# Query sketches of batch 0 on 32x64 tiles, with the heads of a pair swapped by half groups, and a new order

## The chip, the cores and the metric

The kernel runs on one core of a Trainium2 chip. The metric is device time in microseconds, as the median of three runs. The profile is of one further execution of the same program.

## What is computed

Polynomial-sketch attention without softmax, followed by a feed-forward stage (FFN). Batch is 4, heads 4, sequence 1088, head dimension 32, sketch size r = 8; the FFN has 4352 tokens, width 128 and inner width 2048.

```python
def phi(x):                                   # 8 x 8 = 64 features per token and head
    a = np.einsum('rd,bhsd->bhsr', S1, x)
    b = np.einsum('rd,bhsd->bhsr', S2, x)
    return np.einsum('bhsi,bhsj->bhsij', a, b).reshape(*x.shape[:-1], r * r)
q_p, k_p = (phi(q), phi(k))
kv = np.einsum('bhsf,bhsd->bhfd', k_p, v)
z = np.sum(k_p, axis=2)
num = np.einsum('bhsf,bhfd->bhsd', q_p, kv)
den = np.einsum('bhsf,bhf->bhs', q_p, z)[..., None] + 1e-06
# x = (num / den), heads side by side, as 4352 tokens of 128
r = np.maximum(x @ w_in, 0.0)
out = (r * r) @ w_out
```

## The kernel before

The kernel builds a graph of named operations and then emits them in the order of a list, `PLAN`. Each word of the list is `name:engine` and, where it allocates, `:slot`. Every engine works through its own operations in the order in which they stand in the list; an operation at the head of an engine's queue that waits for another engine holds all that stand behind it there. DMA issues take their place in the queue of SP, ACT (ScalarE) or POOL (GpSimd). A word `+12` puts twelve filler matmuls (L328) into TensorE's queue. The list was written out by a planner, which also picks engines where an operation has several (`r`, `g`, `kve`, `ab`, `xe`, `vp`, some `qp`) and the slots of PSUM and SBUF.

The names, for batch b:

- `ldk`, `ldq`, `ldv`: loads of k, q and v (L366 to L392). `vin` has two buffers, so that v of batch 2 goes where v of batch 0 was.
- `tk`, `tq`: 32x32 block transposes of k and q on VectorE (L417, L419, L541). Batch 0 has q in two parts, `tq0.0` and `tq0.1`.
- `ksk`, `ka`, `kp`: sketches of k on TensorE (L458), a copy of the first factor to SBUF on ScalarE (L467), the product of the two on VectorE, for the last piece of batch 0 on GpSimd (L477).
- `vp`: v copied beside a column of ones (L430, L433). `kv`: key features times v, summed over tokens on TensorE (L497). `kve`: its copies from PSUM to SBUF, by pairs of heads; `kvz` holds the two heads of a pair in their places, `kvs` holds them swapped (L515, L517).
- `qr`, `qa`, `qp`: sketches of q repeated to 64 features per head, copy of one factor (`qa`, L567), product (`qp`, L571).
- `num`, `mx`, `tx`, `xe`: query features times state (L793), division by the denominator on VectorE (L806 to L816), transposes on TensorE (L827), copy to `xT` (L831).
- `m1.n.m`, `r`, `g`, `m2`, `oe`, `st`: FFN block n: first product (L858), ReLU (L870 on ScalarE, L872 on VectorE), square (L883, L885), second product (L900), transpose of the result (L910), store (L929). Blocks have 256, 7 times 512, 256 and 256 tokens; block 0 needs only the first group of batch 0.
- `gate`, `win`, `wout`: three loads each of the FFN weights on the GpSimd queue, converted to bf16 on the way; all wait for the gate, a copy that waits for k of batch 0 (L397 to L404). The first two are half as large as the third.

`MODE` gives each batch its way to make the query features: batch 0 "full", batch 1 "half", batches 2 and 3 "rep".

In mode "full" the groups of batch 0 have 320, 384 and 384 columns (`QGROUPS`). Per group and pair of heads there are two matmuls, one for each factor, on a tile of 64 rows and 128 columns. Their weights `SF` are the repeated sketch matrix under a block mask of the two heads, made on GpSimd (L283, L287). In mode "half" of batch 1 one factor is repeated by DMA (`qr1`, `ab1`, `rd1`), the other by matmuls `qb1` on tiles of 32 rows and 64 columns with the weights `SR` (L693). There the heads of a pair are swapped in every second piece of columns, and `num` takes `kvs` in place of `kvz` for these.

The order around the change, in the list before, by engine from the start to the first FFN evacuation on VectorE:

```
PE  ksk0.0-2 qr0.0 ksk1.1 +3 kv0.0-2 qr0.1 num0.0 ksk1.0 qr1 qr0.2 tx0.0 num0.1 m1.0.1 num0.2 tx0.1 m1.0.3 m1.0.0 kv1.0 tx0.2 m1.0.2 qr2 ...
DVE ST tk0.0 mkz mk ident SK tk0.1 SKs tq0.0 tk1.0 kp0.0 kp0.1 qp0.0.0 qp0.0.1 tq0.1 kp1.1 tq1.0 qp0.1.0-1 mx0.0 kp1.0 xe0.0 qp0.2.0-1 mx0.1 mx0.2 tq2.0 xe0.1 xe0.2 r.0.2
```

Of the kernel before, what the change touches and what calls it, by code (L numbers as in the profile page):

```python
# [43 lines left out]
ldk0.0:SP S0:ACT iota:POOL heat0:PE ldk0.1:SP S1:ACT heat4:PE ldk0.2:SP heat2:PE ldq0.0:ACT ldk1.1:SP heat1:PE warm:ACT ldk1.0:SP heat6:PE heat5:PE  # L44
heat7:PE heat3:PE ldv0.0:SP ST:DVE tk0.0:DVE ldv0.1:SP ldv0.2:SP mkz:DVE mk:DVE gate:POOL win0:POOL ldv0.3:SP ident:DVE SK:DVE ldv0.4:SP tk0.1:DVE
SF:POOL +12 ksk0.0:PE:b0 ldq0.1:SP SKs:DVE ksk0.1:PE:b1 ldq1.1:SP tq0.0:DVE SR:POOL ksk0.2:PE:b2 qr0.0:PE:p3,p5 z0:POOL ka0.2:ACT ka0.1:ACT ka0.0:ACT
ldq1.0:SP tk1.0:DVE ldv1.4:SP kp0.2:POOL ldv1.0:SP qa0.0.1:ACT:A0 qa0.0.0:ACT:A1 kp0.0:DVE ldv1.2:SP ksk1.1:PE:b2 ldv1.3:SP vp0.0:POOL ldv1.1:SP
ka1.1:ACT kp0.1:DVE win1:POOL vp0.1:ACT +3 kv0.0:PE:b0 win2:POOL qp0.0.0:DVE wout0:POOL qp0.0.1:DVE kv0.1:PE tq0.1:DVE z1:POOL kv0.2:PE kp1.1:DVE
wout1:POOL ldq2.0:SP qr0.1:PE:p3,p5 kve0.0:ACT kve0.1:ACT ldq2.1:SP tq1.0:DVE num0.0:PE:b1 qa0.1.0:ACT:A2 qa0.1.1:ACT:A1 qp0.1.0:DVE ksk1.0:PE:b0
ldq3.1:SP qp0.1.1:DVE ldk2.0:SP qr1:PE:b2 ka1.0:ACT mx0.0:DVE:den0 ldv2.2:SP qr0.2:PE:p3,p5 ab1.0:ACT ab1.1:ACT rd1.0.1:SP kp1.0:DVE vp1.0:POOL  # L50
rd1.0.0:SP vp1.1:POOL tx0.0:PE qa0.2.0:ACT:A0 rd1.1.0:SP num0.1:PE:b2 xe0.0:DVE qa0.2.1:ACT:A2 qp0.2.0:DVE ldk2.1:SP wout2:POOL qp0.2.1:DVE
m1.0.1:PE:p0 mx0.1:DVE:den1 rd1.1.1:SP num0.2:PE:b3 r.0.1:ACT:r0 ldk3.1:SP tx0.1:PE mx0.2:DVE:den2 m1.0.3:PE:p4 m1.0.0:PE:p0 r.0.3:ACT:r1 ldk3.0:SP
tq2.0:DVE kv1.0:PE:b6 rd1.3.1:SP r.0.0:ACT:r2 rd1.3.0:SP xe0.1:DVE tx0.2:PE m1.0.2:PE:p4 xe0.2:DVE rd1.2.0:SP g.0.0:ACT:g0 qr2:PE:p0 r.0.2:DVE:r3
rd1.2.1:SP m1.1.2:PE:p2 ab2:ACT ldq3.0:SP g.0.2:DVE:g1 m1.1.3:PE:p4 g.0.1:ACT:g2 wr2.3:SP r.1.2:DVE:R4 m1.1.6:PE:p0 kv1.1:PE r.1.3:ACT tk2.0:DVE
r.1.6:ACT:R6 qb1.0:PE:p2,p4 wr2.2:SP g.0.3:ACT:g3 m2.0.0:PE:b7 qp1.0.0:DVE m1.1.0:PE:p0 ldv2.1:SP kve1.1:DVE kve1.0:ACT m2.0.1:PE kve1.3:DVE ldv2.0:SP
kve1.2:DVE r.1.0:ACT:R2 qp1.0.1:DVE m1.1.4:PE:p2 wr2.1:SP tk3.0:DVE ksk2.0:PE:b6 r.1.4:ACT:R0 wr2.0:SP qb1.1:PE:p4,p0 ldv2.3:SP g.1.3:ACT:G4 m2.0.2:PE
qp1.1.0:DVE m1.1.1:PE:p2 ldv2.4:SP qp1.1.1:DVE m2.0.3:PE m1.1.5:PE:p4 oe0:DVE:osb0 ka2.0:ACT r.1.1:ACT num1.0:PE:p0 kp2.0:DVE rdA2.0:SP r.1.5:ACT
tq3.0:DVE rdB2.0:SP ksk2.1:PE:b2 g.1.1:ACT:G6 num1.1:PE:b3 vp2.1:POOL mx1.0:DVE:den0 ksk3.1:PE:b6 g.1.5:ACT:G0 mx1.1:DVE:den1 qr3:PE:p4 st0.0.1:SP
tx1.0:PE ab3:DVE tx1.1:PE ka2.1:ACT m2.1.0:PE:b7 xe1.0:ACT xe1.1:DVE wr3.1:SP m1.1.7:PE:p4 kp2.1:DVE vp2.0:ACT ldv3.3:SP m2.1.1:PE wr3.2:SP r.1.7:ACT
# [916 lines left out]
```

## Time and profile before

| | |
|---|---|
| median of the runs | 111.94 us (111.84 to 114.46) |
| profiled execution | 111.21 us, of it span 109.4 us |
| granted TensorE clock | 1.0 |
| TensorE busy | 102.8 us (94%) |
| VectorE busy | 92.3 us (84%) |
| ScalarE busy | 85.2 us (78%) |
| GpSimd busy | 23.5 us (21%) |
| moved by DMA | 16.33 MB |

The span runs from the first to the last instruction. Busy time of TensorE counts pipelined matmuls to their modelled end. In the views by time a row gives the start, the length, the engine, the line, the operation, the operands and the count; a note in brackets at its end is the idle time just before it, with what ended it. Neighbouring rows of one engine may overlap a little, so the distance of two starts is the better price of an instruction that follows another without a gap.

### The profile page before, as it was taken

What the parts mean: (1) busy time and instruction counts of PE and PEld (TensorE: products, weight loads), DVE (VectorE), ACT (ScalarE), POOL (GpSimd) and SP (SyncE); (2) the same over time, 40 slices, a digit from 0 to 9 for tenths busy, and PEclk for the clock granted to TensorE, in tenths of its full rate; (3) what the DMA queues carried; (4) which work ended last, traced back from release to release, by engine and by line L of the source; (5) the groups of instructions that cost most, each with busy time, mean ns of one, the idle gap of its engine ahead of it and who ended that gap; (6) DMA issues with size and microseconds to landing.
All of it is one profiled execution on the core that took longest, in us unless ns stands there. A gap on an engine that the chain in (4) does not pass through costs nothing.

```text
span 109.4 us, 3331 instructions
## 1 busy us (share of the span) xinstructions
PE 102.8 (94%) x1343; PEld 61.8 (57%) x1343; DVE 92.3 (84%) x141; ACT 85.2 (78%) x105; POOL 23.5 (21%) x45
## 2 busy tenths in 40 slices
PE   7999999999989999999999989999999999999940
PEld 2365864875646955555854435558544544657620
DVE  0199999999899989987998999987999999888540
ACT  0507246399999989998999999991789999999900
POOL 1257918000002103394320505500000000000000
PEclk9999999999999999999999999999999999999999
DMA  1999999999973777546596554450022033143252
GB/s 31 274 327 303 300 208 311 311 267 297 205 247 91 210 210 210 168 116 193 160 235 181 175 151 78 68 96 6 0 46 41 6 57 51 21 75 68 39 88 48
DMA packets 29727, 16.33 MB, mean 149 GB/s; under 512 B 20368, under 2 KB 26896, under 8 KB 29712
## 3 DMA queue, kind: packets, MB, share of 16 engines
q1 hardware_dynamic: 27744, 14.82, 51.7%
q0 software_dynamic: 992, 1.05, 5.8%
q10 hardware_dynamic: 976, 0.26, 1.2%
q8 instruction: 10, 0.16, 0.6%
q14 instruction: 5, 0.04, 0.1%
HBM read 13.27 MB, written 2.79 MB: 147 GB/s over the span
## 4 chain that ended last, share of the span: by engine, by line
PE 62%; DMA 14%; ACT 8%; SPq 6%; DVE 4%; issue 2%; ACTq 1%; POOL 1%; DVEq 0%; POOLq 0%
PE psum L858 20%; PE psum L900 18%; PE psum L793 8%; ACT rraw L870 6%; PE psum L497 6%; DMA vin<-in_v_dram 5%; DMA out_dram<-osb 5%; DMA S_sb<-in_S_dram 3%; PE psum L557 3%; SPq L929 2%; PE psum L827 2%; SPq L741 2%; PE psum L711 2%; DMA scr<-ab 2%; ACT graw L883 2%
## 5 line engine op out<-in xcount | busy, mean ns | idle before, releaser
L870 ACT ACTIVATE rraw<-psum 128x1024 bf16<-128x1024 f32 x51 | 49.4, 1030 | 3.0 <-PE psum L858 2.8
L900 PE MATMUL psum<-graw,w_out 128*128 128x512 bf16 (+1 forms) x160 | 39.3, 347 | 0.6
L858 PE MATMUL psum<-xT,w_in 128*128 128x512 bf16 (+1 forms) x160 | 38.8, 348 | 0.4 <-DVE rraw L872 0.4
L885 DVE TENSOR_TENSOR graw<-rraw 128x1024 bf16<-128x1024 bf16 (+1 forms) x30 | 26.8, 922 | 1.3 <-ACT rraw L870 1.2
L883 ACT ACTIVATE graw<-rraw 128x1024 bf16<-128x1024 bf16 (+1 forms) x18 | 25.6, 1437 | 0.2
L858 PEld LDWEIGHTS <-w_in 128*128 128x128 bf16 x160 | 17.4, 114 | 13.0 <-issue 1.3
L900 PEld LDWEIGHTS <-w_out 128*128 128x128 bf16 x160 | 15.0, 97 | 14.4 <-issue 3.4
L872 DVE TENSOR_SCALAR rraw<-psum 128x1024 bf16<-128x1024 f32 x17 | 20.6, 1219 | 1.6 <-PE psum L858 0.8
L754 POOL TENSOR_TENSOR qp<-qp,Bq 128x384 f32<-128x384 f32 (+1 forms) x9 | 11.6, 1297 | 19.6 <-PE psum L858 6.8
L477 DVE TENSOR_TENSOR kp<-psum,ka 128x1024 f32<-128x1024 f32 (+2 forms) x8 | 10.1, 1268 | 0.0
L793 PE MATMUL psum<-kvz,qp 128*64 128x66 f32 (+1 forms) x252 | 9.6, 223 | 0.0
L793 PEld LDWEIGHTS psum<-kvz,qp 128*64 128x64 f32 (+1 forms) x252 | 8.4, 136 | 1.8 <-ACT A L567 0.5
L497 PEld LDWEIGHTS psum<-vp,kp 128*32 128x32 f32 (+1 forms) x432 | 7.2, 118 | 2.5 <-issue 1.0
L910 DVE STREAM_TRANSPOSE osb<-psum 128x512 f32<-128x512 f32 (+1 forms) x10 | 6.3, 633 | 2.4 <-PE psum L900 2.2
L497 PE MATMUL psum<-vp,kp 128*32 128x33 f32 (+1 forms) x432 | 7.9, 207 | 0.2 <-POOL vp L430 0.2
L328 PE MATMUL psum<-const-bfloat16-1.0 128*128 128x512 bf16 x23 | 7.0, 466 | 0.8 <-PEq L960 0.8
L430 POOL COPY vp<-vin 128x512 f32<-128x512 f32 x5 | 3.0, 615 | 21.0 <-DMA vin<-in_v_dram 21.0
L467 ACT COPY ka<-psum 128x128 f32<-128x128 f32 (+3 forms) x9 | 2.3, 274 | 5.7 <-PE psum L458 5.7
L458 PEld LDWEIGHTS psum<-SK,kT 128*64 128x64 f32 x144 | 5.0, 137 | 2.2 <-DVE kvs L517 0.9
L458 PE MATMUL psum<-SK,kT 128*64 128x64 f32 x144 | 5.8, 225 | 0.4 <-DVE kvs L517 0.4
L541 DVE STREAM_TRANSPOSE qT<-qin 128x1088 f32<-128x1088 f32 (+2 forms) x5 | 5.4, 1072 | 0.1
L417 DVE STREAM_TRANSPOSE kT<-kin 128x1024 f32<-128x1024 f32 (+1 forms) x5 | 5.1, 1020 | 0.1
(63 smaller groups left out, 70.7 us busy)
## 6 DMA issues: line engine op xcount, KB each, us to landing
...
```

Of the source, the lines that this page charges most:

```text
L328: nc.tensor.matmul(tiles["b7"][:, 0:n], ones(128), ones(n), start=True, stop=True)
L458: nc.tensor.matmul(o[32 * g : 32 * g + 32 * gw, :, j - j0, :], lhsT, SK.rearrange("p x h r -> p x (h r)"), start=True, stop=True)
L477: (nc.gpsimd if ke == "POOL" else nc.vector).tensor_tensor(out=kp[i][:, j0:j1].rearrange("p j h (x y) -> p (j h) x y", y=R), in0=bb[:, :, ...
L497: nc.tensor.matmul(t[p : p + fw, 33 * (h // 2) : 33 * (h // 2) + 33], kp[i][:, j, h, f : f + fw], vp[i][:, h, j, :], start=(j == 0 and h < ...
L754: (nc.gpsimd if e == "POOL" else nc.vector).tensor_tensor(out=qp[i][:, pr, t0 : t0 + n], in0=qp[i][:, pr, t0 : t0 + n], in1=Bq[i][:, pr, t ...
L793: nc.tensor.matmul(t[32 * cc : 32 * cc + 32 * m, lo:hi], lhsT, We[:, hf] if part == 2 else w[:, part].rearrange("p m d -> p (m d)"), start ...
L858: nc.tensor.matmul(at(hb)[:, step * w : step * w + N], w_in[:, 512 * (ct // E) : 512 * (ct // E) + 512].rearrange("p (c e) -> p e c", e=E) ...
L870: nc.scalar.activation(o, h, ACTF.Relu)
L872: nc.vector.tensor_scalar_max(o, h, 0.0)
L883: nc.scalar.activation(at(gb)[:, 0:w2], r, ACTF.Square)
L885: nc.vector.tensor_tensor(out=at(gb)[:, 0:w2], in0=r, in1=r, op=ALU.mult)
L900: nc.tensor.matmul(at(ob)[:, 0:N], w_out[:, ct, :], at(gb)[:, lo + N * w : lo + N * w + N], start=(ct == 0), stop=(ct == CT - 1))
```

## The change

Batch 0 goes from mode "full" to mode "pe" (which the code has; the functions are unchanged). Per group, the columns are cut in two halves. For each factor, half and head there is one matmul on a tile of 32 rows and 64 columns, with the plain repeated matrix `SR` as weights: 16 matmuls of half the columns in place of 4. In the first half a head writes the PSUM partitions of its own place in the pair, in the second half those of the other, so that the eight tiles of one factor are all different. `SF` is not made any more. For the swapped half `num0` takes `kvs`, so `kve0` has four copies in place of two.

```diff
-MODE = ("full", "half", "rep", "rep")
+MODE = ("pe", "half", "rep", "rep")
```

The sketches that this puts in the place of L557, and their copies and products:

```python
for x in range(2):
    for half in range(2):
        for h in range(H):
            lo = 64 * ((h % 2) ^ half)
            nc.tensor.matmul(
                at(hb[h // 2])[lo : lo + 64, 512 * half + 256 * x : 512 * half + 256 * x + n],
                SR[32 * h : 32 * h + 32, x].rearrange("p x y -> p (x y)"),
                qT[i][32 * h : 32 * h + 32, t0 + n * half : t0 + n * half + n], start=True, stop=True)
```

The list `PLAN` is new as a whole. By engine, the part up to the first FFN evacuation on VectorE:

```
PE   ksk0.0-2 qr0.0 qr1 +3 kv0.0-2 qr0.1 num0.0 ksk1.0 +1 num0.1 qr0.2 tx0.0 ksk1.1 tx0.1 m1.0.2 m1.0.1 num0.2 kv1.0 m1.0.0 m1.0.3 tx0.2 kv1.1 ...
DVE  mkz ST mk tk0.0 tk0.1 SK tq0.0 tq1.0 SKs kp0.0 kp0.1 ident qp0.0.0 ab1.1 tq0.1 kve0.3 kve0.0 qp0.0.1 tk1.0 qp0.1.0-1 mx0.0 kp1.0 mx0.1 qp0.2.1-0 xe0.1 kp1.1 mx0.2 tq2.0 r.0.0
ACT  ka0.0-2 qa0.0.0 vp0.1 qa0.0.1 ab1.0 kve0.1 kve0.2 qa0.1.1-0 ka1.0 qa0.2.1 xe0.0 qa0.2.0 vp1.0 ka1.1 r.0.2 ...
POOL gate win1 wout1 z0 iota SR win0 vp0.0 win2 kp0.2 wout0 z1 vp1.1 wout2 ...          (before: iota gate win0 SF SR z0 kp0.2 vp0.0 win1 win2 wout0 z1 wout1 vp1.0 vp1.1 wout2)
SP   ldk0.0-2 ldq1.1 ldq1.0 ldv0.0-4 ldq0.1 ldk1.0 ldk1.1 ldv2.3 ldv1.0 ldv1.1 ldv2.4 rd1.1.0 ldv1.3 ldv1.2 ldv1.4 ldq2.1 ldq2.0 ...
     (before: ldk0.0-2 ldk1.1 ldk1.0 ldv0.0-4 ldq0.1 ldq1.1 ldq1.0 ldv1.4 ldv1.0 ldv1.2 ldv1.3 ldv1.1 ldq2.0 ...)
```

Over the whole list VectorE has 13 of the 68 `r` in place of 17, and 13 of the squares of 2048 columns in place of 12, 19 of those of 1024 in place of 18; ScalarE has the rest. The groups, tile sizes, buffers and the number of fillers at the start (8, then 15 in the list, in another division) are otherwise the same.

More of the change, by code (lines that the diff above doesn't have):

```diff
@@ L43 @@
 PLAN = """
[L44 to L59, printed above, removed]
@@ L84 @@
[L84 to L87 removed]
+mkz:DVE ldk0.0:SP S0:ACT heat0:PE ldk0.1:SP S1:ACT heat5:PE ldk0.2:SP heat3:PE ldq0.0:ACT ldq1.1:SP heat7:PE warm:ACT ldq1.0:SP heat1:PE heat2:PE
@@ new lines @@
+heat4:PE heat6:PE ldv0.0:SP ldv0.1:SP ldv0.2:SP gate:POOL ST:DVE win1:POOL mk:DVE ldv0.3:SP tk0.0:DVE wout1:POOL ldv0.4:SP tk0.1:DVE z0:POOL ldq0.1:SP
+ldk1.0:SP SK:DVE tq0.0:DVE iota:POOL +11 ksk0.0:PE:b0 SR:POOL ldk1.1:SP tq1.0:DVE ksk0.1:PE:b1 ka0.0:ACT win0:POOL ksk0.2:PE:b2 ka0.1:ACT
+qr0.0:PE:p3,p5 ka0.2:ACT SKs:DVE kp0.0:DVE qa0.0.0:ACT:A0 qr1:PE:b2 vp0.0:POOL vp0.1:ACT win2:POOL kp0.1:DVE +3 kv0.0:PE:b0 kp0.2:POOL qa0.0.1:ACT:A1
+ldv2.3:SP ident:DVE ab1.0:ACT qp0.0.0:DVE ldv1.0:SP kv0.1:PE ab1.1:DVE ldv1.1:SP wout0:POOL tq0.1:DVE ldv2.4:SP kv0.2:PE z1:POOL rd1.1.0:SP kve0.3:DVE
```

67 lines of the change are left out of this document (39 added, 28 removed).

## The prediction

> **What bounds the kernel now.** I read the page first (busy shares and slices), then busy time by stretches, then the order of time on each engine through the first 28 us, since every removed or added instruction lies there.
>
> ```profile
> PE 102.8 (94%) x1343; PEld 61.8 (57%) x1343; DVE 92.3 (84%) x141; ACT 85.2 (78%) x105; POOL 23.5 (21%) x45
> ...
> DMA  1999999999973777546596554450022033143252
> ```
> ```profile
> 10.00:15.00 5.00, 4.82 (x95) 3.29 (x93) 4.93 (x7) 2.37 (x8) 3.48 (x10) 1.00 1.09 294
> ...
> 30.00:35.00 5.00, 4.45 (x68) 2.77 (x66) 4.74 (x9) 5.00 (x6) 0.04 (x1) 1.00 0.63 190
> ...
> 60.00:70.00 10.00, 9.63 (x183) 5.12 (x182) 9.96 (x12) 9.85 (x11) 4.74 (x3) 1.00 0.51 130
> ```
>
> TensorE is busy 94% of the span, but that row counts pipelined matmuls from start to modelled end, so it overstates the need for TensorE. VectorE is the telling column at the front (the columns are TensorE, its weight loads, VectorE, ScalarE, GpSimd): 4.93 of 5 us between 10 and 15 us, while ScalarE has 2.37. The DMA slices stand at 9 from 2.7 to 27 us. So the attention of batch 0, which has to end before the feed-forward stage can run, is held by VectorE's queue with DMA behind it; later all three engines are near full. The order of time shows how tight VectorE is:
>
> ```profile
> 5.00 0.24 DVE L251 STREAM_TRANSPOSE ST<-S_sb 128x64 f32<-128x64 f32 x1 [5.00 <-DMA S_sb<-in_S_dram]
> ...
> 8.05 1.25 DVE L417 STREAM_TRANSPOSE kT<-kin 128x1024 f32<-128x1024 f32 x1
> ...
> 9.35 2.05 DVE L477 TENSOR_TENSOR kp<-psum,ka 128x1024 f32<-128x1024 f32 x2
> 11.32 0.87 DVE L571 TENSOR_TENSOR qp<-psum,A 128x320 f32<-128x320 f32 x2
> 12.11 0.96 DVE L541 STREAM_TRANSPOSE qT<-qin 128x768 f32<-128x768 f32 x1
> 13.00 1.45 DVE L477 TENSOR_TENSOR kp<-psum,ka 128x1280 f32<-128x1280 f32 x1
> 14.52 1.31 DVE L541 STREAM_TRANSPOSE qT<-qin 128x1088 f32<-128x1088 f32 x1
> 15.75 0.98 DVE L571 TENSOR_TENSOR qp<-psum,A 128x384 f32<-128x384 f32 x2
> 16.66 0.15 DVE L814 TENSOR_SCALAR den<-psum 128x12 f32<-128x12 f32 x1
> ...
> 17.59 1.22 DVE L477 TENSOR_TENSOR kp<-psum,ka 128x1024 f32<-128x1024 f32 x1
> 18.80 0.32 DVE L831 COPY xT<-psum 128x320 bf16<-128x320 bf16 x1
> 19.04 1.01 DVE L571 TENSOR_TENSOR qp<-psum,A 128x384 f32<-128x384 f32 x2
> 19.97 0.16 DVE L814 TENSOR_SCALAR den<-psum 128x12 f32<-128x12 f32 x1
> ...
> 24.13 1.23 DVE L872 TENSOR_SCALAR rraw<-psum 128x1024 bf16<-128x1024 f32 x1 [0.15 <-PE psum L858]
> ```
>
> From the first transpose at 5.00 (it waits for the sketch matrices, which stay) to the first FFN evacuation at 24.13 no row of this engine but the last has an idle note, nor have those left out here. The differences of starts are the prices used below: k transpose of batch 1 1.30 (8.05 to 9.35), the two key products 1.97, a pair of query products 0.79 (320 columns) or 0.91 to 0.93 (384), q transposes 0.89 (768) and 1.23 (1088), the key product of 1280 1.5, that of 1024 1.2, a normalisation 0.93 (16.66 to 17.59), the copy of a transposed group 0.24 to 0.32.
>
> ```profile
> 8.19 1.35 PE L557 MATMUL psum<-qT,SF 64*128 64x320 f32 x8
> ...
> 11.21 2.29 PE L497 MATMUL psum<-vp,kp 128*64 128x33 f32 x72 [0.18 <-POOL vp L430]
> 13.43 1.56 PE L557 MATMUL psum<-qT,SF 64*128 64x384 f32 x8
> ...
> 20.10 0.92 PE L793 MATMUL psum<-kvz,qp 128*64 128x66 f32 x24
> 21.04 0.34 PE L827 MATMUL psum<-ident,xs 128*128 128x128 bf16 x3
> ...
> 23.95 1.12 PE L711 MATMUL psum<-qT,SK 128*32 128x272 f32 x16
> ...
> 26.43 1.36 PE L497 MATMUL psum<-vp,kp 128*64 128x33 f32 x40
> 27.71 0.74 PE L693 MATMUL psum<-qT,SR 32*64 32x288 f32 x16
> ...
> 31.53 0.69 PE L693 MATMUL psum<-qT,SR 32*64 32x256 f32 x16
> ```
>
> On TensorE the sketches (L557, qr0.0 and qr0.1; qr0.2 has the size of qr0.1) last 1.35 and 1.56 us, and kv0 takes 2.22 from its start to the next.
>
> **What is removed and added.** (1) *Sketches.* Each group had 4 logical matmuls of 64x128 over n=320 or 384 columns; it gets 16 of 32x64 over 160 or 192. The trace has the new shape in batch 1: L693, 8 matmuls on the same tiles, lasts 0.74 us at 288 columns (27.71) and 0.69 at 256 (31.53). That is 1.56 ns a column and 0.29 fixed. Two such sets make 0.29+2x160x1.56 ns = 0.79 and 0.89 us if they join without a gap (1.08 and 1.18 if the fixed part is paid twice). Saved: 0.56 + 2x0.67 = 1.9 us of TensorE (1.0 at worst); I take 1.9, since the two sets do not depend on each other.
>
> The Trainium skill, "TensorEngine Tiling (Array Packing)", Gotcha 1, speaks against this: different row tiles cannot access one PSUM bank at the same time, and here two heads of a pair write one bank from different row tiles. The rows above disagree: the old form's slope is (1.56-1.35)/64 = 3.3 ns a column for two matmuls in turn, 1.64 for one, and L693 runs 8 matmuls, two row tiles to a bank, at 1.56; taking turns would need 3.3. By the rule the saving would be gone (a rival below).
>
> (2) *SF and its place on GpSimd.* The block mask (L283, L287) goes; GpSimd had it off every wait. No gain. The sketch weights SR now come with ready margin before qr0.0.
>
> (3) *The swapped states.* Half of each group holds the heads swapped, so batch 0 needs kvs as batch 1 does: kve0 is four copies in place of two, two of them now on VectorE. A VectorE one is 0.23 us, a ScalarE one as much (0.45 for two). num0.0 splits one pair of chunks into single ones (two more logical matmuls, under 0.1 us). PSUM copies and products read two half-banks instead of one run, of the same size: no change taken.
>
> ```profile
> L517 DVE TENSOR_SCALAR kvz<-psum 64x66 f32<-64x66 f32 x3 | 0.7, 227 | 0.1
> ```
> ```profile
> 13.60 0.45 ACT L515 ACTIVATE kvz<-psum 64x66 f32<-64x66 f32 x2 [1.96 <-POOL kvs L297]
> ```
>
> (4) *Batch 1's half sketch.* qr1 moves from behind num0.0 to ahead of kv0, tq1.0 ahead of the key products (in the place of tk1.0, which goes behind), and ab1.1 moves to VectorE, about 0.3 us by the nearest VectorE row, the 320-column copy at 18.80. kp1.1 moves from ahead of the second query group to the end of the front; xe0.0 and xe0.2 go to ScalarE (0.3 us each off VectorE, by the same row).
>
> (5) *Loads.* SP sends q of batch 1 where it sent k, and the reverse; equal bytes. ldv2.3 now stands ahead of batch 1's v; it waits until both copies vp0 have read the buffer, and behind it wait ldv1.0 to ldv1.4, the first rd1 loads and ldq2. Those v parts then go out from about 12 to 16 us; DMA still has a backlog, so they should land near 18, ahead of vp1.0 on ScalarE at about 20. No cost, two us of margin. GpSimd sends win1 and wout1 at once after the gate, and win0 at about 8 us, where it sent win0 alone:
>
> ```profile
> 10.54 0.61 POOL L430 COPY vp<-vin 128x512 f32<-128x512 f32 x1 [0.50 <-DMA vin<-in_v_dram]
> ```
> ```profile
> q0 software_dynamic: 992, 1.05, 5.8%
> ```
>
> The weight queue used 5.8% of 109.4 us on all engines, 6.35 us for 1.05 MB, hence 0.79 us for a piece as large as wout1. These pieces compete with batch 0's v, for which the copy vp0.0 waited until 10.54. Call the delay of v **d**: at least 0 (a small piece trickles beside it anyway) and at most 1.6 (wout1 and win0 both served ahead of it). I take 0.4, half of one piece. The Trainium skill, "DMA: Bandwidth & Descriptors", Queues, rings and completion order, says that an engine takes turns between queue rows; then pieces lined up in the one GpSimd row add no share and d would be 0, which puts the sum below at 112.2. No run here shows it yet.
>
> **The walk.** VectorE, by the prices above: without two small instructions (about 0.1 each) and with 1.23 in place of 1.30, the key products begin at about 9.1 instead of 9.35. Then 1.97, one query product 0.40, ab1.1 0.3 and tq0.1 0.89 bring it to 12.7. Next in its queue stands kve0.3, which needs the end of kv0.2. TensorE can start kv0 at 11.2+d (it waits for vp0 and finds the key products ready), ends 2.2 later, and the copy starts at 13.6+d, as ScalarE's did at 13.60. So VectorE **idles 0.9+d us**, where the old order gave it kp1.1 and had the copies on ScalarE. Behind the waiting copy are kve0.0, the second query product (num0.0 waits for it), tk1.0, and all that follows. After it: two copies 0.46, product 0.40 (14.45+d), tk1.0 1.30, products 0.91 (16.7+d), mx0.0 0.93, kp1.0 1.2, mx0.1 0.93, products 0.93 (20.7+d), xe0.1 0.3, kp1.1 1.5, mx0.2 0.93, tq2.0 1.23: the first FFN evacuation stands at 24.7+d against 24.13. VectorE is **0.6+d later** in the same state.
>
> TensorE: m1.0.1 and num0.2 wait for the products ending at 20.7+d; behind them come kv1.0, two m1.0, tx0.2 and kv1.1. The old order has the same from num0.2 at 20.10 to the end of kv1.1 at 27.71, and in between also qr2 and three m1.1 (23.95 to 26.43, 2.48 us) and tx0.1 (0.34): the common part is 4.8 us, so kv1.1 ends at 25.5+d. For the same work the old order stands at 27.71-2.48 = 25.2. TensorE is **0.3+d later** in spite of 1.9 us less work: the saved time becomes waiting for VectorE. With d=0.4 the sum is +0.7.
>
> **After the front** TensorE's work is the same in both. VectorE's is not. By the plan lists it loses 4 evacuations at 1.22, and gains one square of 2048 at 1.28 and one of 1024 at 0.68; smaller moves cancel to within 0.3. That is 2.9 us less. ScalarE gains 4 at 1.03, loses one square of 1.91 and one of 1.06, and gains some 0.2 in small moves: about +1.4.
>
> ```profile
> L870 ACT ACTIVATE rraw<-psum 128x1024 bf16<-128x1024 f32 x51 | 49.4, 1030 | 3.0 <-PE psum L858 2.8
> ...
> L872 DVE TENSOR_SCALAR rraw<-psum 128x1024 bf16<-128x1024 f32 x17 | 20.6, 1219 | 1.6 <-PE psum L858 0.8 <-ACT graw L883 0.6
> ...
> L885 DVE TENSOR_TENSOR graw<-rraw 128x2048 bf16<-128x2048 bf16 x12 | 15.2, 1284 | 0.3 <-ACT rraw L870 0.3
> L883 ACT ACTIVATE graw<-rraw 128x2048 bf16<-128x2048 bf16 x8 | 15.1, 1910 | 0.1
> ...
> L885 DVE TENSOR_TENSOR graw<-rraw 128x1024 bf16<-128x1024 bf16 x18 | 11.7, 682 | 1.0 <-ACT rraw L870 1.0
> L883 ACT ACTIVATE graw<-rraw 128x1024 bf16<-128x1024 bf16 x10 | 10.5, 1059 | 0.1
> ```
>
> So VectorE's 1.0 us of delay can be made good behind the front, but TensorE's cannot, except out of its waits. Those that show (0.55 of 5 us from 30 to 35, 0.37 of 10 from 60 to 70) come to 0.9; the new order will have its own. I take the exchange as 0, with -0.9 to +1.0. The profiled execution took 111.2 us (span 109.4 and 1.8 around it), so this one goes to 111.9; the median of the runs is 0.7 higher, 111.94. Against the median: **112.6 us**, own range 111.4 (d=0, the waits gone) to 114.0 (d=0.8, one more us of waits).
>
> **Rivals.**
> *A, the lighter engines pay: 110.4.* For it: 1.9 us less on TensorE at 94% busy, 2.9 less on VectorE, which has 9.96 of 10 us at 60 to 70. With d=0 the front costs +0.3, and if the visible waits (0.9) and a third of what VectorE drops (0.9) come off TensorE's path, 111.94+0.3-1.8 = 110.4. Against it: the removed matmuls lie where VectorE sets the pace.
> *B, the wait at kve0.3 grows: 114.1.* One mechanism: v of batch 0 lands late behind wout1 and win0 (d=1.6), and VectorE stands with everything behind kve0.3. Its delay is 0.6+1.6 = 2.2, and where VectorE sets the end this is passed on whole: 111.94+2.2 = 114.1. It takes the forecast's place from about d = 0.8, one whole piece. For it: DMA is full from 2.7 us. Against it: the same queue carried win0 beside v before.
> *C, row tiles take turns: 113.1.* qr0.1 then costs 0.29+4x192x1.56 ns = 1.49, nearly as before; it would stand 0.6 longer between kv0 and num0.0, giving up to 112.6+0.5. The L693 rows speak against it.
>
> **How the numbers follow.** Forecast 0.52, A 0.23, B 0.21, C 0.04. The likeliest gives 112.6. A change of 2% (2.24 us; about what a measurement of this kernel tells from none) means under 109.7 or over 114.2. A falls below 109.7 in four of ten cases (0.10); B above 114.2 in half (0.11), the forecast's tail adds 0.06. So faster 0.10, same 0.73, slower 0.17. The range takes in A's middle and B a little beyond its price: 110.3 to 114.9.
>
> **What would show it.** Right: sketch rows of batch 0 (32x64 tiles) lasting 0.8 to 1.2 us a group; on VectorE an idle note of about 1 us before an L517 copy near 13 to 14 us, released by TensorE's L497; the first FFN evacuation on VectorE later than 24.13; L872 busy 4 to 5 us less; vp0.0's start near 10.9. Wrong: no such idle note (kv0 early, or d negative), a first L858 row before 19.5 us, sketch rows of 1.4 us and more (C), a start of vp0.0 past 12 (B), or TensorE waits of several us behind 30 us, which the walk doesn't reach.

## The result, and the profile after

The changed kernel took **115.65 us** (median of 6 runs, 114.82 to 118.22), the kernel before 112.59 beside it (6 runs, 111.59 to 114.46): **slower, ratio 1.029, 95% interval 1.020 to 1.038**. Ratios here leave out runs that took over 1.5% longer than the fastest run of the same kernel beside them. The profiled execution took 115.98 us with a span of 114.1.

The page of the changed kernel: the shares of the engines, and the evacuations on ScalarE (L870) and VectorE (L872).

```profile
PE 103.4 (91%) x1419; PEld 62.6 (55%) x1419; DVE 90.4 (79%) x139; ACT 86.8 (76%) x108; POOL 21.3 (19%) x43
...
L870 ACT ACTIVATE rraw<-psum 128x1024 bf16<-128x1024 f32 x55 | 53.7, 1039 | 5.1 <-PE psum L858 3.3
...
L872 DVE TENSOR_SCALAR rraw<-psum 128x1024 bf16<-128x1024 f32 x13 | 15.8, 1219 | 2.7 <-PE psum L858 1.7
```

All shares fell though the work is nearly the same: the added time is waiting, on all engines. The changed matmuls are not where it is. TensorE's order of time in the changed kernel shows them at the price that was forecast:

```profile
8.66 0.80 PE L587 MATMUL psum<-qT,SR 32*64 32x160 f32 x32
...
11.79 2.29 PE L497 MATMUL psum<-vp,kp 128*64 128x33 f32 x72
...
15.28 0.91 PE L587 MATMUL psum<-qT,SR 32*64 32x192 f32 x32 [1.19 <-DVE qT L541]
```

VectorE's order of time in the changed kernel, up to the transpose of k of batch 2:

```profile
7.49 0.51 DVE L541 STREAM_TRANSPOSE qT<-qin 128x320 f32<-128x320 f32 x1 [0.41 <-DMA qin<-in_q_dram]
8.93 1.31 DVE L541 STREAM_TRANSPOSE qT<-qin 128x1088 f32<-128x1088 f32 x1 [0.93 <-DMA qin<-in_q_dram]
10.17 0.21 DVE L271 COPY SKs<-SK 128x16 f32<-128x16 f32 x2
10.29 2.08 DVE L477 TENSOR_TENSOR kp<-psum,ka 128x1024 f32<-128x1024 f32 x2
12.29 0.84 DVE L303 TENSOR_SCALAR ident<-iot 128x128 bf16<-128x128 int32 x1
...
14.24 0.98 DVE L541 STREAM_TRANSPOSE qT<-qin 128x768 f32<-128x768 f32 x1 [0.26 <-DMA qin<-in_q_dram]
15.14 0.19 DVE L517 TENSOR_SCALAR kvs<-psum 64x66 f32<-64x66 f32 x1
15.92 0.22 DVE L517 TENSOR_SCALAR kvz<-psum 64x66 f32<-64x66 f32 x1 [0.59 <-ACT kvs L515]
...
26.60 1.18 DVE L872 TENSOR_SCALAR rraw<-psum 128x1024 bf16<-128x1024 f32 x1
...
32.74 1.25 DVE L417 STREAM_TRANSPOSE kT<-kin 128x1024 f32<-128x1024 f32 x1 [2.24 <-DMA kin<-in_k_dram]
```

Four transposes wait for their loads (0.41, 0.93, 0.26 and 2.24 us), the identity matrix stands in the middle of the front and lasts 0.84, and the first evacuation is at 26.60, against 24.13 before.

The ruler for what follows is the start of the output transposes `oe0` to `oe9`, one for each FFN block: `oe0` closes the front, `oe9` the work. Here are `oe0`, `oe1`, `oe6` and `oe9` on VectorE, first before:

```profile
33.85 0.43 DVE L910 STREAM_TRANSPOSE osb<-psum 128x256 f32<-128x256 f32 x1
47.04 0.72 DVE L910 STREAM_TRANSPOSE osb<-psum 128x512 f32<-128x512 f32 x1
...
93.71 0.72 DVE L910 STREAM_TRANSPOSE osb<-psum 128x512 f32<-128x512 f32 x1
...
105.37 0.45 DVE L910 STREAM_TRANSPOSE osb<-psum 128x256 f32<-128x256 f32 x1 [0.69 <-PE psum L900]
```

Then after:

```profile
36.83 0.44 DVE L910 STREAM_TRANSPOSE osb<-psum 128x256 f32<-128x256 f32 x1
50.38 0.70 DVE L910 STREAM_TRANSPOSE osb<-psum 128x512 f32<-128x512 f32 x1
...
97.46 0.71 DVE L910 STREAM_TRANSPOSE osb<-psum 128x512 f32<-128x512 f32 x1
...
110.00 0.45 DVE L910 STREAM_TRANSPOSE osb<-psum 128x256 f32<-128x256 f32 x1 [0.69 <-DMA out_dram<-osb]
```

The front is 2.98 us longer (36.83 against 33.85), the part behind it 1.65 (73.17 against 71.52). What waits behind the front is seen in TensorE's table of waits from 33 to 111 us. Before:

```profile
PE psum L858 <- DVE rraw L872: 0.4, 1, 0.4
```

After:

```profile
PE psum L458 <- DVE kT L419: 1.3, 1, 1.3
PE psum L900 <- DVE graw L885: 0.7, 2, 0.5
PE psum L497 <- DVE den L814: 0.7, 1, 0.7
PE psum L900 <- DVE osb L910: 0.2, 1, 0.2
PE psum L793 <- ACT rraw L870: 0.2, 1, 0.2
```

The first of these lies at 34.13, still in the front, behind the late load of k. The others are one ring of waits at 69 to 76 us, three small waits at 98 to 110, and one of 0.15 at 50.5.

The same milestones do not hold the same work in both lists, so the ruler needs a correction. Ahead of `oe0` TensorE does m1.1.4 and ksk2.0 in the old list; the new one does ksk2.1 there and leaves m1.1.4 and ksk2.0 for later. Behind `oe6` the new list has m1.7.5, m1.7.7 and m1.8.0 in place of m1.8.2. Here is the stretch from `oe0` to `oe9`, first before, then after; behind its length stand the busy times of TensorE, its weight loads, VectorE, ScalarE and GpSimd:

```profile
33.85:105.37 71.52, 70.48 (x882) 41.62 (x881) 64.65 (x86) 65.32 (x70) 13.27 (x13) 1.00 0.43 105
36.83:110.00 73.17, 71.07 (x877) 41.84 (x873) 63.20 (x86) 66.63 (x72) 12.41 (x15) 1.00 0.45 107
```

Of the 1.65 us, 0.59 is TensorE's busy time, that is work which the old list does ahead of `oe0`; TensorE's idle time grew by 1.06 (1.04 to 2.10). The front of the new list is 2.98 us longer although it does that much less.

### The profile page after: what moved, and what is told of

Same layout as the page of the kernel before. It is cut to its first block, busy times and chain, and to the rows that moved or that the text cites. A ratio compares the mean times of both kernels' runs of the same rounds, so it can differ in the third digit from the quotient of the medians.

```text
span 114.1 us, 3476 instructions
## 1 busy us (share of the span) xinstructions
PE 103.4 (91%) x1419; PEld 62.6 (55%) x1419; DVE 90.4 (79%) x139; ACT 86.8 (76%) x108; POOL 21.3 (19%) x43
## 4 chain that ended last, share of the span: by engine, by line
PE 27%; DMA 21%; DVE 21%; SPq 12%; ACT 11%; issue 3%; POOL 1%; ACTq 0%; POOLq 0%
DMA vin<-in_v_dram 12%; PE psum L900 11%; PE psum L858 10%; ACT rraw L870 9%; DVE graw L885 8%; SPq L680 5%; DVE rraw L872 4%; PE psum L793 3%; DVE kp L477 3%; DMA qin<-in_q_dram 3%; DMA S_sb<-in_S_dram 3%; SPq L379 3%; SPq L929 3%; DVE osb L910 2%; DMA kin<-in_k_dram 2%
## 5 line engine op out<-in xcount | busy, mean ns | idle before, releaser
L870 ACT ACTIVATE rraw<-psum 128x1024 bf16<-128x1024 f32 x55 | 53.7, 1039 | 5.1 <-PE psum L858 3.3
L858 PE MATMUL psum<-xT,w_in 128*128 128x512 bf16 (+1 forms) x160 | 38.3, 348 | 0.1
L885 DVE TENSOR_TENSOR graw<-rraw 128x1024 bf16<-128x1024 bf16 (+1 forms) x32 | 28.6, 923 | 1.5 <-ACT rraw L870 1.4
L883 ACT ACTIVATE graw<-rraw 128x1024 bf16<-128x1024 bf16 (+1 forms) x16 | 22.9, 1439 | 0.2
L872 DVE TENSOR_SCALAR rraw<-psum 128x1024 bf16<-128x1024 f32 x13 | 15.8, 1219 | 2.7 <-PE psum L858 1.7
L754 POOL TENSOR_TENSOR qp<-qp,Bq 128x384 f32<-128x384 f32 (+1 forms) x9 | 10.2, 1158 | 23.0 <-PE psum L858 10.7
L328 PE MATMUL psum<-const-bfloat16-1.0 128*128 128x512 bf16 x23 | 8.0, 508 | 0.8 <-PEq L960 0.8
L430 POOL COPY vp<-vin 128x512 f32<-128x512 f32 x4 | 2.5, 613 | 24.6 <-DMA vin<-in_v_dram 24.6
```

What stands on the lines that cost most here:

```text
L754: (nc.gpsimd if e == "POOL" else nc.vector).tensor_tensor(out=qp[i][:, pr, t0 : t0 + n], in0=qp[i][:, pr, t0 : t0 + n], in1=Bq[i][:, pr, t ...
L858: nc.tensor.matmul(at(hb)[:, step * w : step * w + N], w_in[:, 512 * (ct // E) : 512 * (ct // E) + 512].rearrange("p (c e) -> p e c", e=E) ...
L870: nc.scalar.activation(o, h, ACTF.Relu)
L872: nc.vector.tensor_scalar_max(o, h, 0.0)
L883: nc.scalar.activation(at(gb)[:, 0:w2], r, ACTF.Square)
L885: nc.vector.tensor_tensor(out=at(gb)[:, 0:w2], in0=r, in1=r, op=ALU.mult)
```

## The experiments

All times of the ruler, in us. "Old" and "new" name the list. A cross marks a profile in which the granted clock dips below 0.9 in slices of the front; its front is not compared, but it is back at 9 tenths before `oe0`, so the stretches behind can be. The ratios hold within a batch of runs only: the runs of the kernel before that they are taken against average 111.9 us beside e1 to e4, 111.8 beside e5 to e7, 112.9 beside e9 to e12 and 111.4 beside e13 to e15. e9 and e13 are one kernel and have 1.020 and 1.036.

| run | list: front, behind | tiles | `oe0` | oe0-oe1 | oe1-oe6 | oe6-oe9 | oe0-oe9 | ratio, 95% |
|---|---|---|---|---|---|---|---|---|
| before | old | old | 33.85 | 13.19 | 46.67 | 11.66 | 71.52 | |
| e8, before again | old | old | 35.49 | 13.19 | 46.74 | 11.66 | 71.59 | |
| changed | new | new | 36.83 | 13.55 | 47.08 | 12.54 | 73.17 | 1.029, 1.020 to 1.038 |
| e1 | old | new | 36.01 x | 13.19 | 46.61 | 11.66 | 71.46 | 1.012, 1.000 to 1.024 |
| e2 | new | old | 36.78 x | 14.19 | 46.91 | 12.54 | 73.64 | 1.042, 1.027 to 1.056 |
| e3 | new, k of batch 2 early | new | 37.12 x | 14.19 | 46.91 | 12.55 | 73.65 | not given |
| e4 | new, wout1 late | new | 37.03 x | 14.85 | 46.45 | 12.55 | 73.85 | 1.022, 1.008 to 1.035 |
| e5 | new, then old | new | 39.69 x | 13.59 | 46.24 | 11.66 | 71.49 | 1.049, 1.042 to 1.056 |
| e6 | old, then new | new | 37.78 x | 13.39 | 47.30 | 12.54 | 73.23 | 1.026, 1.017 to 1.036 |
| e7 | new, ident early | new | 35.91 | 14.19 | 47.14 | 12.54 | 73.87 | 1.034, 1.027 to 1.041 |
| e9 | new, ring | new | 39.04 x | 14.19 | 46.60 | 12.54 | 73.33 | 1.020, 1.010 to 1.030 |
| e13 | new, ring | new | 35.49 | 14.18 | 46.59 | 12.55 | 73.32 | 1.036, 1.011 to 1.061 |
| e10 | new, ring, ident, k early | new | 35.36 | 13.37 | 46.60 | 12.55 | 72.52 | 1.007, 0.995 to 1.019 |
| e14 | new, tail | new | 35.67 | 14.18 | 46.84 | 11.74 | 72.76 | 1.033, 1.014 to 1.052 |
| e15 | new, all repairs | new | 36.96 x | 14.18 | 46.59 | 11.75 | 72.52 | 1.032, 1.013 to 1.052 |
| e11 | old, state copies late | new | 34.25 | 13.19 | 48.02 | 11.66 | 72.87 | 1.000, 0.991 to 1.008 |
| e12 | e11, copies on ScalarE | new | 35.74 | 13.19 | 46.28 | 11.67 | 71.14 | 1.009, 0.998 to 1.020 |

**Tiles or list? (e1, e2)** e1 keeps the list before and takes the new tiles:

```diff
-MODE = ("full", "half", "rep", "rep")
+MODE = ("pe", "half", "rep", "rep")
-  SF:POOL
+  kve0.2:ACT kve0.3:ACT      (behind kve0.1:ACT)
```

> The old order with the new tiles alone: mode pe for batch 0, no block mask SF, two more copies of the state (kve0.2 and kve0.3, both on ScalarE behind kve0.1). Theory O (the loss is in the new order, in its loads above all): within 1% of before, 111.4 to 113.0 us by the same scale on which before has 112.6, the sketch rows 0.8 to 0.95 us a group, num0.0 starting at or before 14.9 us. Theory T (tiles and swapped states cost): 114.5 us or more, slower than before by over 2%.

e2 takes the new list with the old tiles:

```diff
-MODE = ("pe", "half", "rep", "rep")
+MODE = ("full", "half", "rep", "rep")
+  SF:POOL
-  kve0.2:ACT kve0.3:DVE
```

> The new order with the old 64x128 tiles for batch 0: SF made on GpSimd just ahead of SR, two copies kve0 in place of four. Theory O: as slow as the changed kernel or a little slower, 115.0 to 117.0 us. Theory T: back near before, 112.0 to 113.5 us.

Measured: the new tiles in the old list 114.95 us, ratio 1.012; the old tiles in the new list 116.49, ratio 1.042. So most of the loss goes with the list, and the new tiles take nothing back. The four runs of e1 lie far apart (113.3 twice, 116.6 and 117.0), and its median is outside the range of theory O. In e1 VectorE stood 0.56 us at 17.88 for a sketch copy on ScalarE that the two additional state copies had pushed back; e11 below mends that.

**Single suspects in the front (e3, e4, e7).** e3 sends k of batch 2 ahead of q of batch 2, since the changed kernel waited 2.24 us for it:

```diff
+  ldk2.0:SP ldk2.1:SP        (ahead of ldq2.1:SP)
```

> The changed kernel with the two loads of k of batch 2 moved in SP's queue to just ahead of ldq2.1, that is ahead of the loads of q of batch 2 and of the rd1 loads. If the wait of 2.24 us of VectorE for this k at 32.7 us sets the end: 1.5 to 2.2 us off 115.7, about 113.8, and no idle note at that transpose. If it is covered by other late work (rd1 is pushed back by as much), less than 0.5 us: 115.2 to 116.

e4 sends wout1 late again, as the list before did:

```diff
-  wout1:POOL                 (behind win1)
+  wout1:POOL                 (behind z1)
```

> The changed kernel with the load wout1 moved in GpSimd's queue from the second place to behind the memsets z1 (its place before the change). If wout1 delays the early loads: the notes at the q transposes (0.41 and 0.93 us) shrink by half or more, the key products start near 9.5 in place of 10.29, and the time falls by 0.5 to 0.9 us to about 115.0. If q of batch 1 is late because its 557 KB lie ahead of it in SP's queue and not because of wout1: key products still at 10.1 or later, time within 0.3 us of 115.7.

Measured: 116.54 and 115.74 us. In e3 the wait for k of batch 2 is gone and the median is no lower; in e4 the q transposes still waited 0.44 and 1.04 us and the key products began at 10.37. So neither load order by itself shows a gain. Both profiles have a cross, so a few tenths of a microsecond in the front are not excluded.

e7 makes the identity matrix at the start, as the list before does:

```diff
+  iota:POOL                  (first on GpSimd)
+  ident:DVE                  (behind mk)
-  ident:DVE                  (behind kp0.1)
```

> The changed kernel with the index pattern (iota) first in GpSimd's queue and the making of the identity (ident) right behind mk on VectorE, in place of behind the key products. Lock theory (ident, 0.23 us before the change and 0.84 to 1.56 us in the four runs with the new list, stands still until GpSimd's product kp0.2 ends): ident takes 0.2 us again, VectorE's front is 0.5 to 1.2 us earlier from the first query product on, the time 0.5 to 1.2 us lower. Rival (it only waits for something that is late anyway): the query product starts no earlier than 13.0 us and the time stays.

Measured 115.58, and on VectorE the row of e7 is:

```profile
6.06 0.23 DVE L300 TENSOR_SCALAR ident<-iot 128x128 bf16<-128x128 int32 x1
```

0.23 us again, where the changed kernel has 0.84. The reason stands on GpSimd in the changed kernel:

```profile
10.85 0.61 POOL L430 COPY vp<-vin 128x512 f32<-128x512 f32 x1 [2.50 <-DMA vin<-in_v_dram]
...
11.95 1.08 POOL L477 TENSOR_TENSOR kp<-kb,ka 128x512 f32<-128x512 f32 x1
```

The product `kp` ends at 13.03, and the identity at 13.13: it waited for it. The front of e7 closed 0.9 us earlier (35.91), but the part behind grew to 73.87 and the time stayed. That the 0.9 us came from the identity is not shown. In e7 VectorE also did not wait for k of batch 2, for which it stood 2.24 us in the changed kernel. And e13 and e14 below leave the identity in its place; in e13 its row is

```profile
12.46 0.21 DVE L300 TENSOR_SCALAR ident<-iot 128x128 bf16<-128x128 int32 x1
```

and in e14 it took 0.22, since GpSimd's product began only after it (13.07 and 12.74). Their fronts closed at 35.49 and 35.67, as early as that of e7. So whether the identity loses time depends on when GpSimd gets v of batch 0, and what it is worth at the end stays open. What grew behind the front called for a test of that part alone.

**Front or behind? (e5, e6)** e5 follows the new list until m1.1.6 and then the old one; e6 follows the old list (new tiles) until m1.1.2 and then the new one. Both pay at the seam between the lists: VectorE waits 1.25 us for TensorE at 30.56 in e5 and 1.60 at 30.76 in e6.

> The changed kernel's list as far as the first product of FFN block 1 (ahead of m1.1.6), and from there the old list less what is already done; the squares g.0.0 and g.0.1 change SBUF slots. Theory F (the loss is in the front of the new list): as slow as the changed kernel, and from the first output transpose oe0 to the last one 73.2 us or more. Theory K (the new list loses 1.7 to 2.3 us behind block 0, since its four runs so far need 73.2 to 73.9 us from oe0 to oe9, the old list 71.5 twice): oe0 to oe9 back to 71.4 to 72.0, and 1.2 us or more off the changed kernel.

> The mirror image: the old list with the new tiles as far as block 1 (ahead of m1.1.2), then the new list less what is done; ab2 stands first in it, and three SBUF slots differ. Theory K: oe0 near 34 to 36 us as with the old list, oe0 to oe9 73.0 to 73.9, 1.5 to 2.3 us slower than the new tiles in the old order. Theory F: oe0 to oe9 below 72.3 and the time within 0.8 us of the new tiles in the old order.

First and last output transpose of e5:

```profile
39.69 0.43 DVE L908 STREAM_TRANSPOSE osb<-psum 128x256 f32<-128x256 f32 x1
...
111.18 0.45 DVE L908 STREAM_TRANSPOSE osb<-psum 128x256 f32<-128x256 f32 x1 [0.69 <-PE psum L898]
```

And of e6:

```profile
37.78 0.44 DVE L908 STREAM_TRANSPOSE osb<-psum 128x256 f32<-128x256 f32 x1
...
111.01 0.45 DVE L908 STREAM_TRANSPOSE osb<-psum 128x256 f32<-128x256 f32 x1 [0.69 <-DMA out_dram<-osb]
```

71.49 with the old list behind, 73.23 with the new one, whatever list led there. By the ruler the new list itself is longer behind block 0, by 1.65 us in the changed kernel and by up to 2.35 in other runs of it, 0.6 of it the work named above. The times do not confirm it: e5 took 117.20 us, more than the changed kernel, where theory K had at least 1.2 less, and e6 116.15. Both fronts closed late, at 39.69 and 37.78, with a cross and the seam in them.

**How much is luck of the run? (e8)** The kernel before, profiled again.

> The kernel before, word for word, profiled once more. If the late loads of the front (q0.0 by 0.4 to 0.6 us, the load that stands behind k of batch 0 by 0.9 to 1.2) come from the chip and not from the change: notes of DMA waits at the q transpose and the k transpose of batch 1 also here, oe0 at 35 to 36 us and the end later by the same amount. If they come from the change: none of them, oe0 at 33.9 as in the first profile.

112.92 us. Two rows of VectorE explain why it is 1.7 longer than the first profile of the same kernel:

```profile
8.90 1.25 DVE L415 STREAM_TRANSPOSE kT<-kin 128x1024 f32<-128x1024 f32 x1 [1.03 <-DMA kin<-in_k_dram]
...
28.98 1.25 DVE L415 STREAM_TRANSPOSE kT<-kin 128x1024 f32<-128x1024 f32 x1 [0.79 <-DMA kin<-in_k_dram]
```

The kernel before waits for its early loads too, and the delay goes to the end whole (`oe0` +1.64, `oe9` +1.71). Against this profile the changed one is 3.0 us longer in span: 1.34 up to `oe0`, 1.58 behind it, 0.1 at the end. That is close to the 2.9% of the runs.

**Which waits behind the front? (e9, e13, e10, e14, e15)** The ring, in the changed kernel's order of time on all engines:

```profile
69.31 1.00 POOL L754 TENSOR_TENSOR qp<-qp,Bq 128x384 f32<-128x384 f32 x1 [9.24 <-PE psum L858]
69.54 1.85 DVE L885 TENSOR_TENSOR graw<-rraw 128x2048 bf16<-128x2048 bf16 x1 [0.27 <-ACT rraw L870]
71.42 1.94 ACT L870 ACTIVATE rraw<-psum 128x1024 bf16<-128x1024 f32 x2 [1.00 <-DVE graw L885]
73.25 0.30 ACT L467 COPY ka<-psum 128x160 f32<-128x160 f32 x1
73.58 1.49 DVE L477 TENSOR_TENSOR kp<-psum,ka 128x1280 f32<-128x1280 f32 x1 [1.56 <-ACT ka L467]
75.22 0.90 PE L497 MATMUL psum<-vp,kp 128*32 128x33 f32 x80 [0.67 <-DVE den L814]
```

VectorE's square takes 1.85 us in place of 1.22 beside GpSimd's product; ScalarE waits for its buffer 1.00; the copy `ka3.1` stands behind that evacuation; VectorE waits 1.56 for the copy, and TensorE 0.67 for VectorE. Each engine is late for the next. One word moved breaks it:

```diff
-  r.5.6:ACT                  (ahead of ka3.1:ACT)
+  r.5.6:ACT                  (behind ka3.1:ACT)
```

> The changed kernel with one operation moved on ScalarE: the evacuation r.5.6, which in the changed list waits 1.00 us for VectorE's square (71.42), goes behind the state copy ka3.1, for which VectorE waits 1.56 us (73.58) and TensorE 0.67 us after it (75.22). Theory K1 (the ring of waits at 69 to 76 us is what the new list loses behind block 0): the copy runs at about 71.4 in place of 73.25, the product kp at about 71.9 in place of 73.58, the two waits of 1.56 and 0.67 us go, and the distance from the first to the last output transpose falls from 73.2 to 73.9 us in the runs of the new list to 72.5 or less; median about 1 us below the 115.7 of the changed kernel. Rival K2 (the loss is spread over the order, and a wait removed at one place returns at the next): the waits named go or shrink, but the distance stays at 73.0 to 73.9 and the ratio to the kernel before stays at 1.02 to 1.035.

> The same edit as the run with the ring reordered (r.5.6 behind ka3.1 on ScalarE), for a profile at the full clock. Theory K1 (the ring is a part of the loss behind block 0): distance from the first to the last output transpose 72.4 to 72.8 us, as in the run with all repairs (72.52), in place of 73.17 to 73.87; the tail waits of 0.2 to 0.5 us on TensorE stay. Rival K2 (that 72.52 came from the front's repairs, not from the ring): 73.2 to 73.9.

Measured: 115.37 and 115.38 us. VectorE's wait for the copy shrinks to 0.30 us, TensorE's 0.67 is gone, and oe1 to oe6 takes 46.60 and 46.59 as in the old list (47.08 in the changed kernel, 46.91 in e2 and e3). The order on ScalarE is what makes VectorE wait, not the late square: in e4, with the order unmended, the square takes 1.23 there, and VectorE still waits 1.56. The whole distance did not shrink as expected (72.5 or less in e9, 72.4 to 72.8 in e13); 73.33 and 73.32 lie in the range of rival K2, because oe0 to oe1 took 14.19 and 14.18 here. In the profiles with the new list there, that stretch has two values: 13.4 to 13.6 (changed kernel, e6, e10) and 14.2 or more (the others). Two squares of VectorE stand right ahead of `oe1` in the new list, and the rows of VectorE and GpSimd in e14 show what happens to them:

```profile
46.77 1.23 DVE L882 TENSOR_TENSOR graw<-rraw 128x2048 bf16<-128x2048 bf16 x1
47.12 1.72 POOL L751 TENSOR_TENSOR qp<-qp,Bq 128x384 f32<-128x384 f32 x1 [0.96 <-DMA Bq<-scr]
47.91 2.02 DVE L882 TENSOR_TENSOR graw<-rraw 128x2048 bf16<-128x2048 bf16 x1
```

Between two squares of VectorE, GpSimd's product gets its data from a DMA and starts. It then ends 0.84 us after the first square (48.00 to 48.84), and the second square ends 1.09 us after the product (49.93): they take turns, and `oe1` stands in VectorE's queue behind the late square. In e10 the product came after both squares had begun:

```profile
46.46 2.36 DVE L882 TENSOR_TENSOR graw<-rraw 128x2048 bf16<-128x2048 bf16 x2
...
47.72 3.88 POOL L751 TENSOR_TENSOR qp<-qp,Bq 128x384 f32<-128x384 f32 x3 [1.59 <-DMA Bq<-scr]
```

There two squares took 2.36 us, and the stretch 13.37. All profiles sort themselves this way: in the eight long ones the two squares take 3.17 us or more, in the three short ones 2.36 to 2.53, and the old list has a single square at this place. So the moment at which GpSimd gets its data, in most of these by a DMA, decides over some 0.8 us. TensorE is busy in nearly all of the long stretch (14.13 of 14.18 us in e14); its own wait comes 4 us behind `oe1`, in most of the long ones alike:

```profile
53.96 0.59 PE L897 MATMUL psum<-graw,w_out 128*128 128x512 bf16 x2 [0.89 <-ACT graw L880]
```

That the late square is the cause of this wait is read from the rows; no run took the collision away by an edit. The sum from `oe0` to `oe6` shows that both losses are paid:

| oe0 to oe6 | two squares in 3.17 us or more | two squares in 2.53 us or less |
|---|---|---|
| new list, ring as it was | 61.02 to 61.33 (e2, e3, e4, e7, e14) | 60.63, 60.69 (changed, e6) |
| new list, ring mended | 60.77 to 60.79 (e9, e13, e15) | 59.97 (e10) |

The ring is worth 0.2 to 0.7 us and the collision 0.3 to 0.8. With both out the new list is at 59.97, where the old one is in most profiles (59.80 to 59.93; 61.21 in e11, 59.47 in e12).

e10 takes the ring, the identity and the loads of e3 together.

> The changed kernel with three repairs of its list at once: the evacuation r.5.6 behind ka3.1, the identity matrix made at the start (0.23 us in place of 0.84), and the loads of k of batch 2 ahead of those of q of batch 2. Theory K1: the front gains 0.6 to 1.0 us (first output transpose at about 36, as with the identity alone, 35.9), the part behind it 0.8 to 1.5 us, so a median of 113.5 to 114.3 and a ratio to the kernel before of 1.01 to 1.015. Rival K2: the front's gain is lost behind it, as with the identity alone (35.91 then 73.87), and the ratio stays at 1.025 to 1.035.

115.0 us, ratio 1.007 with an interval that holds 1, and 72.52 behind the front: the best version of the new list by its profile. The part behind came as the first theory expected, the median did not (113.5 to 114.3). It is not told apart from the kernel before, but the runs beside it were longer than in the other batches, and 0.8 us of its gain is the collision that happened not to occur.

e14 mends the last stretch alone:

```diff
-  r.8.0:DVE (ahead of g.7.6)      g.9.1:ACT (ahead of r.9.3)
+  r.8.0:DVE (behind g.7.7)        g.9.1:DVE (behind r.9.2)
```

> The changed kernel with two operations moved in the last 14 us: the evacuation r.8.0, for which VectorE waits 0.81 us (101.08) ahead of squares that TensorE needs, goes behind the squares g.7.6 and g.7.7; and the square g.9.1 goes from ScalarE, where it stands ahead of the last evacuation r.9.3, to VectorE, which idles there. Theory K3 (the waits of the last stretch are part of what the new list loses): TensorE's waits of 0.24 and 0.47 us go, distance from the first to the last output transpose 0.5 to 0.7 us shorter than 73.2 to 73.9, so 72.5 to 73.3, and the stretch from oe6 to oe9 12.0 us or less in place of 12.54; ratio to the kernel before 1.02 to 1.025. Rival K4 (the waits come back at the neighbours: r.8.0 frees its PSUM later and the last blocks' products wait for it): oe6 to oe9 stays at 12.4 to 12.7.

`oe6` and `oe9` of e14:

```profile
96.69 0.71 DVE L907 STREAM_TRANSPOSE osb<-psum 128x512 f32<-128x512 f32 x1
...
108.43 0.45 DVE L907 STREAM_TRANSPOSE osb<-psum 128x256 f32<-128x256 f32 x1 [0.69 <-PE psum L897]
```

11.74 us in place of 12.54, a little more than the 0.5 to 0.7 I expected, and that although by the list it holds more of TensorE's work than the old 11.66 (79 matmuls in the changed kernel, 76 before). The stretch is a property of the list to the hundredth: 11.66 or 11.67 in all six profiles with the old list there, 12.54 or 12.55 in the nine with the new one unmended. The time does not show the gain: 116.13 us and ratio 1.033, where 1.02 to 1.025 was expected.

e15 has all five repairs.

> The new list with all five repairs (identity early, loads of k of batch 2 early, the ring, the two of the tail). Theory K1 and K3 together: first output transpose at 35.3 to 36.3, distance to the last 71.8 to 72.1, median 113 to 114 in the measure of the runs, ratio to the kernel before 0.995 to 1.005: the loss was in the order, and nothing of it in the tiles. Rival (something else in the new list costs a constant, such as 16 more sketch products of TensorE behind block 0, 0.4 us): distance 72.3 or more and ratio 1.005 to 1.015.

Behind the front each piece came as it should (46.59, 11.75), with the collision (14.18), so 72.52 and not 71.8 to 72.1; the rival's 72.3 or more was met too. The time, 115.34 us and ratio 1.032, missed both expectations: its front closed at 36.96, with the granted clock at 5, 5 and 7 tenths in the sixth to eighth of 40 slices:

```profile
PEclk9999955799999999999999999999999999999999
```

Why the clock dips there in many runs stays open (last section). So the ring and the tail are shown by repair, in the stretches of the profiles; the collision is shown by profiles that have it and others that do not. No version of the new list was level with the old one in all stretches at once, and no repair by itself is seen in the time.

**The new tiles in a mended old list (e11, e12).** e11 moves kve0.2 and kve0.3 behind the sketch copy that VectorE waited for:

```diff
-  kve0.2:ACT kve0.3:ACT      (behind kve0.1)
+  kve0.2:ACT kve0.3:ACT      (behind qa0.1.1, then num0.0:PE)
```

> The old list with the new query sketches of batch 0, and the two additional state copies kve0.2 and kve0.3 on ScalarE behind the sketch copy qa0.1.1 in place of ahead of qa0.1.0, so that VectorE's query product no longer waits 0.56 us for ScalarE (17.88 in the run of the old list with the new tiles). Theory T1 (the new sketches by themselves are worth nothing, and those copies cost the old list about half a microsecond): the note of 0.56 goes, first output transpose 0.3 to 0.6 us earlier than 36.0, distance to the last transpose 71.5 as in all old lists, ratio to the kernel before 1.00 to 1.01. Rival T2 (shorter sketches on TensorE do help once the copies are out of the way): first output transpose below 35.2 and ratio 0.985 to 0.995. Rival T3: the products of batch 0 (num0.0, now behind the copies on TensorE) wait for the copies as long as the product of VectorE did, and nothing changes: ratio about 1.012.

e12 puts xe0.0, xe0.1 and xe0.2 on ScalarE as well.

> As the run with the state copies moved, and the three copies of transposed attention output of batch 0 (xe0.0, xe0.1, xe0.2: 0.33 us and 0.66 us for two on VectorE) on ScalarE, where ScalarE had 2.6, 1.0, 0.9 and 0.7 us of idle time in this stretch. Theory T4 (what bounds the first 26 us is VectorE, and whatever leaves it there comes off the end one for one, since the order behind block 0 adds a constant 71.5 us): first evacuation by VectorE 0.7 to 1.0 us earlier than 26.46, first output transpose at 34.6 to 35.3, distance to the last 71.5, ratio to the kernel before 0.985 to 0.995. Rival T5 (ScalarE is as late as VectorE there, its evacuations of block 0 give the time back): first output transpose at 35.5 to 36.0 and ratio 1.00 to 1.01.

e11: 112.98 us, ratio 1.000 (0.991 to 1.008). The 0.56 us are gone, and no loss against the kernel before is left, though the interval overlaps that of e1. The tiles bring nothing either, as expected of sketches that VectorE hides. Its oe0 to oe9 of 72.87 broke the constant of 71.5: TensorE waited 0.41 and 0.79 us for VectorE's evacuations at 66 and 72 us, so a front that ends early (34.25) is not sure to be passed on whole. e12: 114.22, ratio 1.009; VectorE now waited 0.73 us for TensorE at its first evacuation, and the front closed no earlier than in e8. What left VectorE came back as this wait. Neither beats the kernel before.

## Why the prediction was wrong, point by point

The forecast was 112.6 us, range 110.3 to 114.9, most likely no change; it came to 115.65, slower by 2.9%.

1. **Sketches: right.** 0.80 and 0.91 us a group, 0.79 and 0.89 forecast. Rival C, taking turns, would have shown 1.49 for the second group. Where the Trainium skill, "TensorEngine Tiling (Array Packing)", "Gotcha 1: PSUM Pressure", speaks against two row tiles in one bank, the measurement decides: two row tiles to a bank ran at full rate. The saving was worth nothing at the end, as forecast (e11).
2. **Delay d of v: right in this profile, by luck of the loads.** vp0.0 began at 10.85 for 10.54 before, d = 0.3 for 0.4 taken. That is one profile: over all of them this start lies between 10.37 and 12.30 with the old list in front and between 10.74 and 12.59 with the new one, so d can't be told from 0. Rival B does not explain the result: the changed kernel's own start was early, and in e7, with 12.41, TensorE waited 0.77 us for this copy and the front still closed earlier than in the changed kernel.
3. **Start of the key products: wrong, 10.29 for 9.1.** The step took every load as timely, because the one profile of before shows no late one. Two loads of q cost 0.41 and 0.93 us; e8 shows 1.03 for the kernel before. Over all profiles of either list this start lies between 8.94 and 11.35.
4. **The walk from there: nearly right, 16.3 for 16.0 us to the first evacuation** (15.6+d). But the idle note at the first L517 copy is absent: with VectorE 1.2 us late, kv0 was ready for it. In its place came two things that the walk had left out. The identity was taken out at the start ("without two small instructions") and never put back where the new list has it; there it cost 0.84, not 0.1, since it meets GpSimd's product. And a state copy waited 0.59 us for another one on ScalarE.
5. **Loads of the later batches: wrong.** The step priced the loads behind ldv2.3 at no cost and did not follow them to k of batch 2. That came 2.24 us late to VectorE, and TensorE lost 1.3. What this costs at the end is not shown: e3 gained nothing, e7 and e13 did not wait for it and closed the front 0.9 and 1.3 us earlier, but so did e14 (1.2) with a wait of 1.59, and e8 had 0.79 of the same kind.
6. **Behind the front, the exchange taken as 0: the step that failed.** It counted what the engines have to do (VectorE 2.9 us less, ScalarE 1.4 more) and took the waits as even. L872 did fall by 4.8 us (20.6 to 15.8), as forecast. But the time is set by who waits for whom: +1.65 us by the ruler, outside my -0.9 to +1.0. Of this 1.06 is more idle time of TensorE and 0.59 is work that the old list does ahead of `oe0`; so as a price of waiting the term was 1.06 for 0. By stretches the 1.65 is 0.36 from oe0 to oe1, 0.41 to oe6 (the ring; 46.6 when mended), 0.88 to oe9 (the tail; 11.74 when mended). I had said that "TensorE waits of several us behind 30 us, which the walk doesn't reach" would prove it wrong: they came to 1.8 us behind `oe0` (0.4 before), and that is where it failed.

Against the kernel before in the same runs the forecast was +0.7 and the result +3.06. By the ruler 1.65 of the miss of 2.4 lies behind the front, and e5 and e6 show that it follows the list. With the moved work put where the old list has it, about 1.1 is behind the front and 1.3 in it. In the front the late loads (point 3 and 5) and the identity (0.6, point 4) are seen in the rows, but no run shows what either is worth by itself. Rival A failed for the same reason as point 6: a lighter VectorE pays nothing where the order lets it wait.
